# Blocks of tokens backwards in the second half of each layer, and the weights' lower halves on VectorE

## The chip, the cores and the metric

The kernel runs on one core of a Trainium2 chip. The metric is device time in microseconds (us), the median of three runs. A profile is taken of one further execution; its views count from the first instruction (the span).

## The reference

Linear attention, then two gated feed-forward layers one after the other, all in float32:

```python
def phi(x):                                  # per head, 128 features
    proj = x @ w_phi
    proj = proj - max(abs(proj), over features)
    return concatenate([exp(proj), exp(-proj)])
q_p, k_p = phi(q), phi(k)                    # 4 batches, 8 heads, 576 tokens, 64 wide
x = (q_p @ (k_p^T v)) / (q_p @ sum(k_p) + 1e-6)      # 2304 tokens x 512
x = (silu(x @ w_gate)     * (x @ w_val))  @ w_out    # layer 1, 512 -> 1536 -> 512
x = (sigmoid(x @ w_gate2) * (x @ w_val2)) @ w_out2   # layer 2
```

## The kernel before

**Arithmetic.** A float32 matmul is made of three matmuls of a shorter float type: each operand is cut into an upper half (a cast) and a lower half (the source minus the upper half), and upper x upper, upper x lower and lower x upper are summed in PSUM. Cutting one operand is therefore a cast on ScalarE and a subtraction on another engine; `halves` (line 196) does both. The gate and value products go by Strassen's scheme with 7 block products instead of 8, so that weights and tokens first go through sums of quarters (`sums`, on VectorE), and the results are put together by ScalarE copies (`keep`) and VectorE additions (`add`).

**Staging.** Each layer is run in two halves of 768 hidden columns, so there are four of them, `hh` = 0 to 3, and three turns between them: 0 to 1 and 2 to 3 inside a layer, 1 to 2 from layer to layer. In each half the loop runs over five blocks of tokens (`BLOCKS`: four of 512 and, in third place, one of 256) and inside a block over three pairs of weight columns (`p` = 0, 1, 2). One (hh, block, p) is a unit. Within a unit of a full block the order of the products is `ORDER[1]` = 1, 5, a, b, 6, 3, c, 7, 2, d, 4. The digits are Strassen products (each 2 x 6 matmuls of 256 columns); the letters are the output matmuls (`accumulate`) of the unit before, in four groups of six matmuls of 512 columns, `a` and `b` for its first hidden part (f = 0), `c` and `d` for its second (f = 1).

**PSUM hand-overs.** Products 1, 6, 7 and 4 add up in one bank (tag `a`). ScalarE must have copied it after 1 and after 6 (`keep`) before the next of them may write, and VectorE must have added it after 7 (`add`, line 634, `c<-a,c`) before 4 may write. The output sums of a block stay in the four banks of tags `c` and `d` until `out_sum` empties them.

**What a turn brings.** The halves of three weight pairs are kept on the chip in two tiles per pair (`w0h`, `w0l` and so on, with `o0h`, `o0l` for the output weights). When a unit is the last reader of its pair, `plan_slot` loads the pair of the next half (`a<-wf`, `o0l<-wfo`), sums and cuts it. In turn 0 to 1, 1 to 2 and 2 to 3 the subtraction of the 1024-wide weight piece is on VectorE, and those of the 768-wide one (the Strassen sums, source `s`) and of the output weights are on GpSimd (`SE`, line 814). Tokens have two buffers (`x0`, `x1`); before each block `plan_x_block` loads it (`b<-xo`), sums (lines 568 to 571) and cuts it (`xl`). In the first half of a layer each block's output sums are copied out and stored (`part<-o`); in the second they are loaded back (`o<-part`) and added.

**Order.** Every step has a planned time (`at(t, ...)`), steps are written in the order of these times, and a scheduling layer then sets the order on each engine. On the chip an engine runs its instructions strictly in that order. DMAs are all issued from SyncE's one queue, in order too. Loads and stores share four staging buffers (`piece`, tag `raw`).

Of the kernel before, what the change touches and what calls it, by code (L numbers as in the profile page):

```python
# [58 lines left out]
BLOCKS = [(0, 512), (512, 512), (2048, 256), (1024, 512), (1536, 512)]  # L59
NPAIR = 3  # L60


# [44 lines left out]
def body(ctx: ExitStack, tc: tile.TileContext, qT, kT, v, w_phi2, wpk, out):  # L107
# [87 lines left out]

    def halves(eng, hi, lo, src, act):
        act = act or anchor["early"]
        with tc.issue_after(anchor["act" if act else "dve"].ins):
            (nc.scalar.copy if act else nc.vector.tensor_copy)(hi, src)  # L199
        eng.tensor_tensor(out=lo, in0=src, in1=hi, op=ALU.subtract)  # L200

    def plan_slot(t, hh, p, eng, gap=3.0, out=14.0):
        l, q = hh // 2, (hh % 2) * NPAIR + p
# [18 lines left out]
        def split(w, m):  # L222
            if (hh, p) not in wts:
                wts[hh, p] = [pools[f"w{p}"].tile([P, 2, 2, 7, P], R32, tag=f"w{p}{x}",
                                                  name=f"w{p}{x}{hh}") for x in "hl"]
            d, src = ((slice(0, 4), a), (slice(4, 7), s))[m]
            halves(eng[m], *(x[:, w, :, d] for x in wts[hh, p]), src[w], WA)

# [7 lines left out]
        def split_out():  # L236
            hi, lo = wts[hh, p, "o"]
            halves(eng[2], hi, lo, lo.bitcast(F32), WA)

# [309 lines left out]

    def plan_x_block(t, hh, j, eng, gap):  # L550
        n = BLOCKS[j][1]
# [23 lines left out]
        def split(c, m):  # L575
            if (hh, j) not in xs:
                k = (hh * len(BLOCKS) + j) % 2
                xs[hh, j] = [pools[f"x{k}"].tile([P, 2, 7, NQ], R32, tag=x, name=x)
                             for x in ("xh", "xl")]
            d = ((slice(0, 4), slice(4, 7)) if full else (slice(0, 4, 2), slice(4, 5)))[m]  # L580
            src = b[c] if m == 0 else s[c][:, :3 if full else 1]
            halves(eng[m], *(x[:, c, d] for x in xs[hh, j]), src, XA)

# [6 lines left out]
    def product(r, hh, j, p, w, k):  # L590
# [12 lines left out]
        a, b = (PROD if full else PROD_HALF)[k]  # L603
        wh, wl = (x[:, w, :, a] for x in wts[hh, p])
        xh, xl = (x[:, :, b] for x in xs[hh, j])
        for c in range(2):
# [58 lines left out]
    def accumulate(r, hh, j, p, f, h):  # L665
        n = BLOCKS[j][1]
        wh, wl = (x[:, f] for x in wts[hh, p, "o"])
        uh, ul = r["u", f]
        m = (KC if hh < 2 else n // P) // 2
        for i in range(h * m, h * m + m):  # L670
            if p == 0 and f == 0:
                acc[hh, j, i] = bank(tags[i])
            ps = acc[hh, j, i]
            for m, (a, x) in enumerate(((wh, uh), (wh, ul), (wl, uh))):
                st, sp = p == 0 and f == 0 and m == 0, p == NPAIR - 1 and f == 1 and m == 2
                k = slice(i * P, (i + 1) * P)
                if hh < 2:
                    nc.tensor.matmul(ps[:, :n], a[:, k], x, start=st, stop=sp)  # L678
                else:
                    nc.tensor.matmul(ps, x[:, k], a, start=st, stop=sp)  # L680

    def out_banks(hh, j, k):
# [18 lines left out]
    def out_sum(hh, j, k):  # L701
        o, _ = out_tile(hh, j, k)
        banks, w = out_banks(hh, j, k)
        for m, i in enumerate(banks):
            ps = acc[hh, j, i][:, :w]
            if hh % 2 == 1:
                nc.vector.tensor_tensor(out=o[:, m], in0=ps, in1=o[:, m], op=ALU.add)
            elif m < OA:
                nc.scalar.copy(o[:, m], ps)
            else:  # L710
                nc.vector.tensor_copy(o[:, m], ps)
# [18 lines left out]
    def plan_out(t, r, hh, j, p, f, h):  # L730
# [3 lines left out]
        t += 6 * n / NQ * PT  # L734
        if p == NPAIR - 1 and f == 1:
            if hh < 2:
# [3 lines left out]
            for i, k in enumerate(tiles):  # L740
                if hh % 2 == 1:
                    at(t - 8.0, out_load, hh, j, k)
                at(t + 0.1 + 1.2 * i, out_sum, hh, j, k)
                at(t + OS + 1.5 * i, out_store, hh, j, k)
# [53 lines left out]
    for hh in range(4):  # L798
        begin.append(t)
        for j, (_, n) in enumerate(BLOCKS):  # L800
            if last:
                xprep.append((t, hh, j))
# [8 lines left out]

    S0 = X0 = (nc.vector,) * 3
    V, G = nc.vector, nc.gpsimd
    SE, XE = ((V, G, G), (V, G, G), (V, G, G)), (V, V)
    SG, XG = 2.72, 2.13
# [9 lines left out]
    for j, b in enumerate((0, 1, 3, 2, 3)):  # L825
        for c in range(2):
            plan_norm(ready[b] + NO[j] + 3.0 * c, j, c)
    plan_x_block(ready[0] + NO[0] + X00, 0, 0, X0, 3.0)
    plan_slot(T0 - WO, 0, 0, S0)
    plan_slot(ready["e"] + W1, 0, 1, S0, 1.5)  # L830
    plan_slot(ready["nd"] + W2, 0, 2, (G, G, G))
    for t, hh, j in xprep:
        plan_x_block(t - XL, hh, j, XE, XG)
    for hh in range(1, 4):
        plan_rounds(hh, begin[hh - 1] + RA, begin[hh] - RZ)
        for p in range(NPAIR):
            plan_slot(free[hh - 1, p] + SO, hh, p, SE[p], SG)
    plan.issue()
# [42 lines left out]
```

## Time and profile before

| | |
|---|---|
| median of three runs | 1072.55 us (1068.43 to 1075.91) |
| profiled execution, its own time | 1068.21 us |
| span of the profile | 1066.2 us |
| mean granted TensorE clock over the span | 0.992 |
| TensorE matmul busy | 1023.8 us, 96% |
| VectorE busy | 747.3 us, 70% |
| ScalarE busy | 556.9 us, 52% |
| GpSimd busy | 128.9 us, 12% |

Attention takes about the first 190 us of the span, the two layers the rest. In the views, PE is TensorE, PEld its weight loads, DVE VectorE, ACT ScalarE, POOL GpSimd, SP SyncE; L200 is line 200. A share of busy time is a mean over stages: for the layers read it turn by turn. The granted clock 1.00 is 2.4 GHz and 0.50 is 1.2 GHz.

### The profile page before, as it was taken

The numbers are of one execution on the slowest core, as the hardware profiler recorded it, in microseconds if no ns is written. First come the engines' busy times: TensorE is split into PE (matmuls) and PEld (weight loads), VectorE is DVE, ScalarE is ACT, GpSimd is POOL, SyncE is SP. The second block draws the span as 40 slices with busy tenths as digits, with TensorE's granted clock in tenths as the row PEclk, the third lists the DMA queues.
The fourth block names the chain that finished last, engine by engine and source line by source line (L and its number), as shares of the span: only waits on it lengthen the run. The fifth ranks groups of instructions, "written<-read, shape, count | busy, mean of one in ns | idle before, by whom it ended". The sixth has DMA issues, their size and how long they took to land.

```text
span 1066.2 us, 20722 instructions
## 1 busy us (share of the span) xinstructions
PE 1023.8 (96%) x8344; PEld 918.8 (86%) x8344; DVE 747.3 (70%) x1274; ACT 556.9 (52%) x1006; POOL 128.9 (12%) x109
## 2 busy tenths in 40 slices
PE   7999999997999998999999999999999899999998
PEld 6777776786999888999998888999989799999997
DVE  6988888875766788667757887567577974563433
ACT  5887877633555555534444455465455453332322
POOL 3322330210000014200000133000001230000000
PEclk9999999998999999999999999999999999999999
DMA  7777867648756251436634534154434340340111
GB/s 226 218 242 209 240 191 212 207 137 240 241 169 178 89 190 44 154 110 207 218 130 141 174 111 158 52 188 161 138 116 159 99 144 15 104 134 34 47 40 40
DMA packets 88575, 157.41 MB, mean 148 GB/s; under 512 B 28896, under 2 KB 50592, under 8 KB 88480
## 3 DMA queue, kind: packets, MB, share of 16 engines
q1 hardware_dynamic: 88480, 156.10, 46.9%
q8 instruction: 65, 1.06, 0.4%
q14 instruction: 30, 0.25, 0.1%
HBM read 108.73 MB, written 47.33 MB: 146 GB/s over the span
## 4 chain that ended last, share of the span: by engine, by line
PE 70%; DVE 13%; DMA 10%; ACT 3%; issue 2%; SPq 1%; POOL 0%; DVEq 0%; ACTq 0%
PE a L608 21%; PE b L608 15%; PE c L680 7%; PE d L680 5%; PE d L678 5%; PE c L678 5%; PE d L412 4%; PE a L317 4%; DMA rb<-rden 3%; DMA raw<-wpk 3%; PE c L363 3%; DVE xl L200 2%; DMA b<-xo 1%; DVE c L634 1%; PE b L385 1%
## 5 line engine op out<-in xcount | busy, mean ns | idle before, releaser
L646 ACT ACTIVATE c<-c 128x256 f32<-128x256 f32 x96 | 50.2, 524 | 166.6 <-DVE c L634 166.5
L659 DVE TENSOR_TENSOR ul<-c,uh 128x512 fp32r<-128x512 f32 (+1 forms) x120 | 75.1, 636 | 49.7 <-ACT uh L658 49.0
L628 ACT COPY c<-a 128x512 f32<-128x512 f32 x96 | 56.1, 584 | 86.8 <-PE a L608 77.4
L658 ACT CAST uh<-c 128x512 fp32r<-128x512 f32 (+1 forms) x120 | 68.5, 576 | 61.5 <-DVE c L651 53.6
L634 DVE TENSOR_TENSOR c<-b,c 128x512 f32<-128x512 f32 x96 | 65.6, 684 | 48.9 <-PE b L608 48.9
L608 PE MATMUL a<-xh,w2h 128*128 128x256 f32 x288 | 82.0, 285 | 8.3 <-DVE c L634 8.3
L608 PE MATMUL a<-xh,w1h 128*128 128x256 f32 x288 | 81.5, 283 | 7.2 <-DVE c L634 7.2
L608 PE MATMUL a<-xh,w0h 128*128 128x256 f32 x288 | 81.0, 281 | 1.4 <-ACT c L628 1.4
L608 PE MATMUL a<-xh,w2l 128*128 128x256 f32 x288 | 81.5, 283 | 0.0
L608 PE MATMUL a<-xl,w2h 128*128 128x256 f32 x288 | 81.5, 283 | 0.0
L608 PE MATMUL a<-xh,w1l 128*128 128x256 f32 x288 | 81.0, 281 | 0.0
L608 PE MATMUL a<-xl,w1h 128*128 128x256 f32 x288 | 80.9, 281 | 0.0
L608 PE MATMUL a<-xh,w0l 128*128 128x256 f32 x288 | 80.5, 279 | 0.0
L608 PE MATMUL a<-xl,w0h 128*128 128x256 f32 x288 | 80.4, 279 | 0.0
L163 ACT ACTIVATE raw<-raw 128x512 int32<-128x512 uint32 x72 | 48.7, 678 | 60.1 <-DMA raw<-wpk 54.6
L651 DVE TENSOR_TENSOR c<-c 128x256 f32<-128x256 f32 x96 | 56.3, 586 | 28.4 <-ACT c L646 27.7
L200 POOL TENSOR_TENSOR w0l<-s,w0h 128x768 fp32r<-128x768 f32 x6 | 12.4, 2059 | 501.0 <-PE b L608 333.3
L167 DVE TENSOR_SCALAR wcv<-wcv 128x512 f32<-128x512 f32 x72 | 32.3, 449 | 54.7 <-ACT wcv L160 54.6
L608 PEld LDWEIGHTS a<-xh,w2h 128*128 128x128 f32 x288 | 55.6, 193 | 11.8 <-DVE c L634 9.6
L200 DVE TENSOR_TENSOR xl<-b,xh 128x1024 fp32r<-128x1024 f32 (+1 forms) x40 | 50.7, 1267 | 20.1 <-ACT xh L199 19.9
L608 PEld LDWEIGHTS a<-xh,w1h 128*128 128x128 f32 x288 | 54.8, 190 | 11.5 <-DVE c L634 9.3
L608 PE MATMUL b<-xh,w1h 128*128 128x256 f32 x224 | 62.3, 278 | 0.0
(181 smaller groups left out, 3500.5 us busy)
## 6 DMA issues: line engine op xcount, KB each, us to landing
raw<-wpk SPq DMA_DIRECT2D x72, 512.0 KB
b<-xo SPq DMA_DIRECT2D x32, 512.0 KB
wf<-wcv SPq DMA_DIRECT2D x48, 256.0 KB
a<-wf SPq DMA_DIRECT2D x24, 512.0 KB
part<-o SPq DMA_DIRECT2D x17, 512.0 KB
o<-part SPq DMA_DIRECT2D x17, 512.0 KB
wfo<-wcv SPq DMA_DIRECT2D x24, 256.0 KB
x<-kT SPq DMA_DIRECT2D x18, 256.0 KB
```

The lines of the kernel that those rows point to most:

```text
L163: nc.scalar.activation(r["lo"].bitcast(I32), r["lo"], AF.Copy, scale=2.0 ** -29)
L200: eng.tensor_tensor(out=lo, in0=src, in1=hi, op=ALU.subtract)
L317: nc.tensor.matmul(ps[:, i * 256:(i + 1) * 256], x[:, i, o:o + P], w, start=(m == 0 and i == 0), stop=(m == 2 and i == 1), skip_group_chec ...
L608: nc.tensor.matmul(o, f[:, c], x[:, c], start=k == first and w == 0 and c == 0 and m == 0, stop=c == 1 and m == 2, skip_group_check=True)
L628: anchor["act"] = nc.scalar.copy(part_of(r, d), parts(r, src))
L634: anchor["dve"] = nc.vector.tensor_tensor(out=c, in0=parts(r, "zy x"[d]), in1=c, op=ALU.add)
L646: nc.scalar.activation(o, g, AF.Silu if hh < 2 else AF.Sigmoid)
L651: nc.vector.tensor_tensor(out=o, in0=v, in1=places(r, j, 0, d)[1], op=ALU.mult)
L658: nc.scalar.copy(hi, v)
L659: nc.vector.tensor_tensor(out=lo, in0=v, in1=hi, op=ALU.subtract)
L678: nc.tensor.matmul(ps[:, :n], a[:, k], x, start=st, stop=sp)
L680: nc.tensor.matmul(ps, x[:, k], a, start=st, stop=sp)
```

## The change

`ROUTE` orders the blocks 0, 1, 2, 3, 4 in halves 0 and 3 and 4, 3, 2, 1, 0 in halves 1 and 2. So the last two blocks of half 0 (3 and 4) are the first two of half 1, in reverse, and so for halves 2 and 3; their cut tokens are still in the two buffers and are used again (`xs[hh, j] = None`). The block at the turn also keeps its output sums in PSUM (`goes_on`): no copy, no store and no load of `part` for it. The turn from layer 1 to layer 2 (1 to 2) prepares its blocks as before. `halves` loses its engine argument: every lower half of tokens and weights is now subtracted on VectorE.

```diff
+ROUTE = ((0, 1, 2, 3, 4), (4, 3, 2, 1, 0), (4, 3, 2, 1, 0), (0, 1, 2, 3, 4))
...
-    def halves(eng, hi, lo, src, act):
+    def halves(hi, lo, src, act):
...
-        eng.tensor_tensor(out=lo, in0=src, in1=hi, op=ALU.subtract)
+        nc.vector.tensor_tensor(out=lo, in0=src, in1=hi, op=ALU.subtract)
...
-                k = (hh * len(BLOCKS) + j) % 2
+                k = (hh // 2 + ROUTE[hh].index(j)) % 2
...
+        if xs[hh, j] is None:
+            xs[hh, j] = xs[hh - 1, j]
...
+            begins, ends = not goes_on(hh, j), not goes_on(hh + 1, j)
             if p == 0 and f == 0:
-                acc[hh, j, i] = bank(tags[i])
+                acc[hh, j, i] = bank(tags[i]) if begins else acc[hh - 1, j, i]
...
+    def goes_on(hh, j):
+
+        return hh % 2 == 1 and ROUTE[hh][0] == j == ROUTE[hh - 1][-1]
...
-            if hh % 2 == 1:
+            if hh % 2 == 1 and not goes_on(hh, j):
                 nc.vector.tensor_tensor(out=o[:, m], in0=ps, in1=o[:, m], op=ALU.add)
...
-        if p == NPAIR - 1 and f == 1:
+        if p == NPAIR - 1 and f == 1 and not goes_on(hh + 1, j):
...
-                if hh % 2 == 1:
+                if hh % 2 == 1 and not goes_on(hh, j):
                     at(t - 8.0, out_load, hh, j, k)
...
-        for j, (_, n) in enumerate(BLOCKS):
-            if last:
+        for i, j in enumerate(ROUTE[hh]):
+            if hh % 2 == 1 and i < 2:
+                xs[hh, j] = None
+            elif last:
                 xprep.append((t, hh, j))
...
-    S0 = X0 = (nc.vector,) * 3
-    V, G = nc.vector, nc.gpsimd
-    SE, XE = ((V, G, G), (V, G, G), (V, G, G)), (V, V)
...
-    plan_slot(ready["nd"] + W2, 0, 2, (G, G, G))
+    plan_slot(ready["nd"] + W2, 0, 2)
```

The order of the matmuls on TensorE stays the same but for two places where three or four of them change places with their neighbours. Three places on VectorE and ScalarE follow. Line numbers in the rows of the changed kernel are its own: L203 there is L200 here, L220 to L223 are L217 to L220, L639 is L634, L656 is L651, L664 is L659, L543 is L540, L202 is L199, L651 on ScalarE is L646, L633 is L628, L663 is L658. In all names `w0` is the weight pair, `x` and `b` tokens, `s` and `t` Strassen sums, `c` a result in the making.

First place: VectorE at the turn 0 to 1, in the unit in which pair 0 of the next half is cut. Before:

```order
L569 TENSOR_TENSOR b<-b 128x256
L570 TENSOR_TENSOR t<-b 128x256
L571 TENSOR_TENSOR t<-b,t 128x256
L634 TENSOR_TENSOR c_5123<-b,c_5123 128x2x256
L568 TENSOR_TENSOR t<-b 128x256
L200 TENSOR_TENSOR w0l_5170<-a,w0h_5169 128x2x512
L200 TENSOR_TENSOR xl<-b,xh 128x1024
L634 TENSOR_TENSOR c_5139<-a,c_5139 128x2x256
```

In this order a token cut (`xl`) stands right ahead of the addition `c_5139<-a` that product 4 waits for. The same place after the change:

```order
L222 TENSOR_TENSOR s<-s,a 128x2x128
L223 TENSOR_TENSOR s<-a,s 128x2x128
L203 TENSOR_TENSOR w0l_5170<-s,w0h_5169 128x2x384
L639 TENSOR_TENSOR c_5123<-b,c_5123 128x2x256
L203 TENSOR_TENSOR w0l_5170<-a,w0h_5169 128x2x512
L203 TENSOR_TENSOR w0l_5170<-s,w0h_5169 128x2x384
L639 TENSOR_TENSOR c_5139<-a,c_5139 128x2x256
```

The tokens' four sums and cut are gone; sums of the next pair and two 768-wide weight subtractions stand in their place.

Second place: VectorE at the turn 1 to 2, one unit later, where pair 1 is cut. Before:

```order
L200 TENSOR_TENSOR xl<-b,xh 128x1024
L200 TENSOR_TENSOR xl<-t,xh 128x768
L200 TENSOR_TENSOR w1l_7666<-a,w1h_7665 128x2x512
L634 TENSOR_TENSOR c_7613<-b,c_7613 128x2x256
L217 TENSOR_TENSOR s<-a 128x2x128
L200 TENSOR_TENSOR w1l_7666<-a,w1h_7665 128x2x512
L218 TENSOR_TENSOR a<-a 128x2x128
L219 TENSOR_TENSOR s<-s,a 128x2x128
L634 TENSOR_TENSOR c_7632<-a,c_7632 128x2x256
```

Here the cuts of tokens and weights share the unit, and the output weights' subtraction is not on this engine. After the change:

```order
L203 TENSOR_TENSOR o0l_7507<-o0l_7507,o0h_7506 128x1024
L203 TENSOR_TENSOR xl<-b,xh 128x1024
L223 TENSOR_TENSOR s<-a,s 128x2x128
L203 TENSOR_TENSOR xl<-t,xh 128x768
L203 TENSOR_TENSOR w1l_7604<-a,w1h_7603 128x2x512
L639 TENSOR_TENSOR c_7551<-b,c_7551 128x2x256
L203 TENSOR_TENSOR w1l_7604<-s,w1h_7603 128x2x384
L221 TENSOR_TENSOR a<-a 128x2x128
L222 TENSOR_TENSOR s<-s,a 128x2x128
L639 TENSOR_TENSOR c_7570<-a,c_7570 128x2x256
```

The subtraction of `o0l`, which waits for a load and a cast, now stands at the head of this row, and one 1024-wide weight subtraction has moved behind the addition `c_7570<-a`.

Third place: VectorE near the start of the layers, where the last token block is normalised (`xraw`, which waits for the load of `rb`) beside the fifth or so unit. Before:

```order
L651 TENSOR_TENSOR c_3619<-c_3619 128x512
L540 TENSOR_TENSOR xraw<-xraw,rb 128x1024
L659 TENSOR_TENSOR ul_3749<-c_3619,uh_3748 128x512
L651 TENSOR_TENSOR c_3634<-a,c_3634 128x256
L659 TENSOR_TENSOR ul_3785<-c_3634,uh_3784 128x512
```

Both lower halves that the output matmuls read (`ul`) stand behind `xraw`. After the change:

```order
L656 TENSOR_TENSOR c_3619<-c_3619 128x512
L179 ISA wcv<-raw,wcv 128x1024
L656 TENSOR_TENSOR c_3634<-a,c_3634 128x256
L664 TENSOR_TENSOR ul_3749<-c_3619,uh_3748 128x512
L543 TENSOR_TENSOR xraw<-xraw,rb 128x1024
L664 TENSOR_TENSOR ul_3785<-c_3634,uh_3784 128x512
```

The first `ul` has moved ahead of `xraw`, the second still stands behind it.

## Rows read from the trace of the kernel before

**Rows 1.** The page, busy time, share of the span, instructions of each engine.
```profile
PE 1023.8 (96%) x8344; PEld 918.8 (86%) x8344; DVE 747.3 (70%) x1274; ACT 556.9 (52%) x1006; POOL 128.9 (12%) x109
```

**Rows 2.** Windows at the turns: length, busy us by engine (instructions), clock, DMA share, GB/s.
```profile
380.00:420.00 40.00, 34.99 (x234) 31.82 (x234) 35.11 (x55) 20.83 (x32) 12.78 (x5) 0.96 0.37 119
600.00:640.00 40.00, 35.61 (x242) 32.62 (x241) 33.54 (x49) 21.61 (x32) 13.10 (x6) 0.96 0.40 131
820.00:860.00 40.00, 34.75 (x235) 31.85 (x235) 34.71 (x51) 22.70 (x33) 14.04 (x7) 0.96 0.26 81
```

**Rows 3.** Waits of TensorE from 240 us: us in total, times, longest.
```profile
PE a L608 <- DVE c L634: 14.2, 6, 3.1
```

**Rows 4.** Timeline, VectorE at turn 0 to 1: start, us, instruction, [idle before <- releaser].
```profile
386.40 0.42 DVE L569 TENSOR_TENSOR b<-b 128x256 f32<-128x256 f32 x1
...
389.49 0.42 DVE L568 TENSOR_TENSOR t<-b 128x256 f32<-128x256 f32 x1 [1.15 <-POOL w0l L200]
...
390.97 2.87 DVE L200 TENSOR_TENSOR xl<-b,xh 128x1024 fp32r<-128x1024 f32 x1
393.77 0.68 DVE L634 TENSOR_TENSOR c<-a,c 128x512 f32<-128x512 f32 x1
...
406.34 2.87 DVE L200 TENSOR_TENSOR w1l<-a,w1h 128x1024 fp32r<-128x1024 f32 x1
...
409.73 1.46 DVE L217 TENSOR_TENSOR s<-a 128x256 f32<-128x256 f32 x1
...
412.92 0.68 DVE L634 TENSOR_TENSOR c<-a,c 128x512 f32<-128x512 f32 x1
```

**Rows 5.** Timeline, GpSimd at turn 0 to 1.
```profile
390.03 2.73 POOL L200 TENSOR_TENSOR w0l<-s,w0h 128x768 fp32r<-128x768 f32 x1 [0.57 <-ACT w0h L199]
...
405.61 5.30 POOL L200 TENSOR_TENSOR w1l<-s,w1h 128x768 fp32r<-128x768 f32 x2 [1.15 <-ACT w1h L199]
```

**Rows 6.** Timeline, TensorE at turn 0 to 1, the two product 4 that waited.
```profile
394.50 0.39 PE L608 MATMUL a<-xh,w1h 128*128 128x256 f32 x1 [1.51 <-DVE c L634]
...
413.65 0.38 PE L608 MATMUL a<-xh,w2h 128*128 128x256 f32 x1 [3.07 <-DVE c L634]
```

**Rows 7.** Line 200 on VectorE: ns minimum, median, maximum of each subtraction.
```profile
L200 DVE TENSOR_TENSOR xl<-b,xh x40: 682/1216/2879, 177.7 to 1000.8; 128x1024 fp32r<-128x1024 f32 x32, 128x512 fp32r<-128x512 f32 x8
...
L200 DVE TENSOR_TENSOR w0l<-s,w0h x2: 944/946/948, 158.2 to 170.5; 128x768 fp32r<-128x768 f32 x2
```

**Rows 8.** Chain of waits, turn 0 to 1: one product, one output group.
```profile
370.49 1.41 PE b L608 x12
371.90 1.39 PE c L678 x6
```

**Rows 9.** Chain of waits, turn 2 to 3: loads and the cast behind one.
```profile
813.31 5.04 DMA a<-wf
...
829.12 7.37 DMA o0l<-wfo
...
836.51 1.05 ACT o0h L199
837.56 0.95 ACT xh L199
```

**Rows 10.** Chain of waits, turn 1 to 2: the tokens' way through memory.
```profile
594.16 5.69 DMA xo<-o
599.87 4.94 DMA b<-xo
```

**Rows 11.** Timeline near the start of the layers, all engines.
```profile
260.20 1.23 DVE L540 TENSOR_TENSOR xraw<-xraw,rb 128x1024 f32<-128x1024 f32 x1 [3.86 <-DMA rb<-rden]
...
261.34 0.68 DVE L659 TENSOR_TENSOR ul<-c,uh 128x512 fp32r<-128x512 f32 x1
...
262.08 0.79 PE L678 MATMUL c<-ul,o0h 128*128 128x512 f32 x1 [4.28 <-DVE ul L659]
```

**Rows 12.** Window near the start of the layers (columns of Rows 2).
```profile
254.00:274.00 20.00, 14.97 (x90) 13.43 (x89) 9.85 (x15) 8.40 (x16) 0.00 (x0) 0.83 0.86 258
```

More of the change, by code (lines that the diff above doesn't have):

```diff
@@ L199, in halves, with plan_slot @@
             (nc.scalar.copy if act else nc.vector.tensor_copy)(hi, src)
-        eng.tensor_tensor(out=lo, in0=src, in1=hi, op=ALU.subtract)
-    def plan_slot(t, hh, p, eng, gap=3.0, out=14.0):
+        nc.vector.tensor_tensor(out=lo, in0=src, in1=hi, op=ALU.subtract)
+    def plan_slot(t, hh, p, gap=3.0, out=14.0):
         l, q = hh // 2, (hh % 2) * NPAIR + p
@@ L226, in split @@
             d, src = ((slice(0, 4), a), (slice(4, 7), s))[m]
-            halves(eng[m], *(x[:, w, :, d] for x in wts[hh, p]), src[w], WA)
+            halves(*(x[:, w, :, d] for x in wts[hh, p]), src[w], WA)
         def load_out():
@@ L237, in split_out @@
             hi, lo = wts[hh, p, "o"]
-            halves(eng[2], hi, lo, lo.bitcast(F32), WA)
+            halves(hi, lo, lo.bitcast(F32), WA)
         for w in range(2):
@@ L548, in plan_norm, with plan_x_block @@
         at(t + 8.0, store)
-    def plan_x_block(t, hh, j, eng, gap):
+    def plan_x_block(t, hh, j, gap):
         n = BLOCKS[j][1]
@@ L581, in split @@
             src = b[c] if m == 0 else s[c][:, :3 if full else 1]
-            halves(eng[m], *(x[:, c, d] for x in xs[hh, j]), src, XA)
+            halves(*(x[:, c, d] for x in xs[hh, j]), src, XA)
         for c in range(2):
@@ L670, in accumulate @@
         for i in range(h * m, h * m + m):
+            begins, ends = not goes_on(hh, j), not goes_on(hh + 1, j)
             if p == 0 and f == 0:
-                acc[hh, j, i] = bank(tags[i])
+                acc[hh, j, i] = bank(tags[i]) if begins else acc[hh - 1, j, i]
             ps = acc[hh, j, i]
             for m, (a, x) in enumerate(((wh, uh), (wh, ul), (wl, uh))):
-                st, sp = p == 0 and f == 0 and m == 0, p == NPAIR - 1 and f == 1 and m == 2
+                st = begins and p == 0 and f == 0 and m == 0
+                sp = ends and p == NPAIR - 1 and f == 1 and m == 2
                 k = slice(i * P, (i + 1) * P)
@@ L827, in body @@
             plan_norm(ready[b] + NO[j] + 3.0 * c, j, c)
-    plan_x_block(ready[0] + NO[0] + X00, 0, 0, X0, 3.0)
-    plan_slot(T0 - WO, 0, 0, S0)
-    plan_slot(ready["e"] + W1, 0, 1, S0, 1.5)
-    plan_slot(ready["nd"] + W2, 0, 2, (G, G, G))
+    plan_x_block(ready[0] + NO[0] + X00, 0, 0, 3.0)
+    plan_slot(T0 - WO, 0, 0)
+    plan_slot(ready["e"] + W1, 0, 1, 1.5)
+    plan_slot(ready["nd"] + W2, 0, 2)
     for t, hh, j in xprep:
-        plan_x_block(t - XL, hh, j, XE, XG)
+        plan_x_block(t - XL, hh, j, XG)
     for hh in range(1, 4):
@@ L836, in body @@
         for p in range(NPAIR):
-            plan_slot(free[hh - 1, p] + SO, hh, p, SE[p], SG)
+            plan_slot(free[hh - 1, p] + SO, hh, p, SG)
     plan.issue()
```

## The prediction

> **What bounds the kernel now.** The busy times come first: TensorE works 96% of the span, VectorE 70%, GpSimd 12% [rows 1]. The matmuls are the same before and after, so the change can only win what TensorE loses by waiting or by a lower clock. Where that is, a table of windows tells: in the undisturbed stretches of the layers TensorE is busy all the time; at each turn, in 40 us, it is busy only 34.99, 35.61 and 34.75 us, and the granted clock is 0.96 instead of 1.00 [rows 2]. Idle time: 5.0 + 4.4 + 5.3 = 14.7 us. The clock: a mean of 0.96 is 0.04 x 40 = 1.6 us of full-speed work lost per turn, 4.8 us in all. Together 19.5 us is what the three turns cost. The list of waits names the releaser: of TensorE's waits from 240 us on, six, 14.2 us together, are for VectorE's addition at line 634, two per turn [rows 3]. They are all product 4 waiting for the addition after product 7 [rows 6].
>
> The timeline shows why the addition is late. VectorE's 1024-wide subtraction takes 1.22 us as a rule (the median is 1216 ns) but 2.87 us twice in this turn [rows 4, 7], and each time GpSimd is in its own subtraction [rows 5]; a quarter-wide sum goes from 0.42 to 1.46 us in the same way, and once VectorE waits 1.15 us for GpSimd outright [rows 4]. Three such stretches and the wait lie in the 24 us ahead of the two late additions: 2 x 1.65 + 1.04 + 1.15 = 5.5 us of VectorE time. So the turns are bound by VectorE, in part by its own work and in part by GpSimd standing in its way.
>
> A second place is the start of the layers: at 260 us VectorE sits 3.86 us before `xraw` until a load lands, the lower half `ul` stands behind it, and TensorE waits 4.28 us [rows 11]; the granted clock there is 0.83 over 20 us [rows 12].
>
> **The change, part by part.**
>
> *Tokens not prepared at turns 0 to 1 and 2 to 3.* Gone per turn, for two blocks of two pieces each: 16 sums of 0.42 us, 4 cuts of 1.22 and 4 of 0.95 us [rows 4, 7], which is 15.4 us of VectorE, 7.7 us of it (one block) in the two units that waited. The casts on ScalarE and four loads of 512 KB go too. In SyncE's queue the weights' loads move up into the places of the token loads. That shortens the wait; I cost it at nothing more.
>
> *PSUM kept over the turn.* Four copies, four additions, two stores and two loads fewer per layer. They lie beside TensorE's work a unit or more from any wait of rows 3: nothing gained, nothing lost.
>
> *Lower halves to VectorE.* Per turn six of 768 and three of 1024 come to VectorE: 6 x 0.95 + 3 x 1.22 = 9.4 us [rows 7], of which in the two units that waited 4 x 0.95 + 1.22 = 5.0 us. Against that stand the 5.5 us above, which end with GpSimd's work. So at turn 1 to 2, where the tokens are still prepared, VectorE's load stays about level; at the other two it falls by 7.7 + 5.5 - 5.0 = 8.2 us, from 35 of 40 us [rows 2] to about 27.
>
> *The two additions at turn 0 to 1, step by step.* First unit: before, `xl` started at 390.97 and the addition at 393.77 [rows 4]. In the new order the four sums that end near 386.40 + 3 x 0.42 = 387.7 are sums of weights, and then come 0.95, the addition after product 3 with 0.68, 1.22, 0.95 and the addition in question with 0.68: 392.2 [rows 4, 7]. Product 4 could have started at 394.50 - 1.51 = 393.0 [rows 6]. No wait is left. Turn 2 to 3 is alike.
>
> Second unit: now VectorE also takes `o0l`, which waits for its load and for a cast; ahead of it in time stands nothing that TensorE needs, behind it two weight subtractions and both additions. Let T be the start of the unit. Output weights can be loaded once their last reader, group d, is done, one product before T, so about T - 1.0. Product 7 starts at T + 4 x 1.41 + 3 x 1.39 = T + 9.8 (products 1, 5, 6, 3 and groups a, b, c), product 4 after products 7, 2 and group d at T + 14.0 [rows 8]. The load takes 5.04 us like its neighbour or 7.37 like the one at turn 2 to 3 [rows 9], which shared the queue with two others. With 7.37: cast done at T + 7.4, `w1h` cast T + 8.5, copy after product 6 done T + 9.1, ahead of product 7. VectorE: `o0l` T + 8.7, 1024 T + 9.9, 768 T + 10.9, addition T + 11.5, 1024 T + 12.7, 768 T + 13.6, the addition product 4 needs at T + 14.3: a wait of 0.3 us. With 5.04 none. I take 0.3 at each of these turns.
>
> *Turn 1 to 2.* The first unit: the tokens come by a store of 5.69 and a load of 4.94 us [rows 10], unchanged; without GpSimd's share the addition lies within a few tenths of product 4: no wait taken. The second unit: between the cast of `o0` and the copy after product 6 ScalarE still has two token casts of 0.95 us [rows 9], 1.9 us more. With 7.37 the copy ends at T + 11.0, 1.2 us after product 7 could start, and the addition for product 4 at T + 15.5. That is a wait of 1.5 us; with 4.94 none. I take 1.5, and keep 1.6 us of lower clock with it, since every turn with waits shows that loss [rows 2].
>
> By the Trainium skill (DMA: Bandwidth & Descriptors, section "Anatomy of one DMA — SWDGE (gpsimd) path") a transfer costs 2.0 us plus its bytes at 436 GB/s, an estimate of 3.2 us for 512 KB, stated for the other issuing path; by it no turn would keep a wait and the sum would be 1068.2 - 19.5 - 5 = 1043.7. The trace does not agree: its loads of that size take 4.94 to 7.37 us.
>
> *The start.* The first `ul` now stands ahead of `xraw`, the second behind. TensorE reads the second only after groups a, b and products 6, 3, that is 2 x 1.39 + 2 x 1.41 = 5.6 us [rows 8] after group a began, half a us ahead of its wait, at 257.3: at 262.9; `xraw` and `ul` end at 260.20 + 1.23 + 0.68 = 262.1. So the wait of 4.28 goes, and with it the clock's loss: 0.17 x 20 = 3.4 us, of which up to 4.28 / 2 = 2.1 fell on idle time, so 1.3, together 5.6. Bounds: 0, if the load of `rb` lands later or another instruction waits in its place, and 5.6. I take 5, near the upper end, since the order shows the step itself. Pair 2 of the first half (5.5 us of subtractions, now on VectorE) falls at 201 to 217 us, where GpSimd's hold was of the same size: nothing.
>
> **The sum.** Turns: 19.5 less 0.3 + 0.3 + 1.5 + 1.6 = 15.8 us won. Start: 5. 1068.2 - 20.8 = 1047.4 for an execution like the profiled one. That one lies 0.2 us under the lowest of the three runs and 4.3 under their median. Runs that lie higher probably lose it in the same waits, which are now fewer, so I add little of it: **1048 us**.
>
> **Rivals.**
> *The gain is given back at turn 1 to 2 and the start (partial).* VectorE there carries tokens and all weights in order; one cast that lands late delays everything behind. If turn 1 to 2 keeps its 6.5 us (a third of 19.5) and the start its 5: 1068.2 - 2 x 6.5 + 0.6 = 1055.8, with the runs' spread up to 1061. For it: VectorE is busy 33.5 of 40 us there already. Against it: GpSimd's hold is gone.
> *The turns are bound by loads, not by VectorE.* Chain pieces of loads end in the late stretches [rows 9, 10]. Then TensorE waits just as long for other instructions: 1064 to 1072. Against it: the loads' buffers come free earlier, and only one of the two waits per turn has a load in its chain.
> *VectorE and ScalarE stuck behind loads (slower).* GpSimd could wait for output weights at no cost; VectorE cannot. Nine such subtractions (o0, o1, o2 at three turns), and at turn 0 to 1 three raw weight pieces that ScalarE now handles ahead of gates, stand in order before TensorE's additions. Each us beyond T + 6.4 costs 1 us at each. To lose 1% beyond the 20.8 won, 31.5 us, the loads would have to take 7.4 + 31.5 / 9 = 10.9 us. The longest row is 7.37. Time then: 1079.
> *The change does less than it says,* since the scheduling layer sets the order: the order shows that GpSimd has no subtraction left in the layers, so this has no chance of its own.
>
> **How the numbers follow.** Within 1% is about what a measurement of this kernel can tell from no change: 1061.8 to 1083.3. Forecast 0.63 (1040 to 1052: all waits and the start gone, or the start's gain missing); partial 0.22 (1052 to 1061); bound by loads 0.11; stuck 0.04. So faster 0.85, same 0.11, slower 0.04. The range leaves out the last two cases: low 1039 (the sum less 3.7 us of waits kept, less the 0.6 between bound and value at the start, less the 4.3 us by which executions stood apart before), high 1061.
>
> **What would show it.** In the windows of the three turns TensorE should be busy over 39 of 40 us with a clock of 1.00 at the first and third. The list of waits should have no six waits for the addition. The 1024-wide subtraction should have a maximum near 1.23 us, GpSimd no subtraction after 175 us. The wait at 262 us should be gone. The prediction is wrong if TensorE waits for `c<-a` or for ScalarE's copy behind `o0h`, `o1h` at the turns, or if `xraw` holds another reader at the start.

## The result and the profile after

The changed kernel took 1046.72 us (median of 6 runs, 1041.87 to 1050.72), the kernel before 1070.93 us in the runs beside it (6 runs, 1068.43 to 1075.91). The ratio is 0.976 with a 95% interval of 0.9734 to 0.9786. The forecast was 1048 us and a range of 1039 to 1061.

The profiled execution of the changed kernel is the longest of its six, 1050.72 us with a span of 1048.9; that of before, with a span of 1066.2, was shorter than all of its timed runs. So the two profiles differ by 17.3 us where the medians differ by 24.2. The page's first part, after, answers to [rows 1]:

```profile
PE 1022.0 (97%) x8344; PEld 919.6 (88%) x8344; DVE 710.7 (68%) x1250; ACT 544.0 (52%) x990; POOL 52.8 (5%) x77
```

There are as many matmuls as before. GpSimd has lost 32 subtractions, but VectorE is busy for less: 710.7 instead of 747.3 us. It took over those 32 and has the tokens of two turns less; and in the layers nothing of GpSimd runs beside it any more.

The windows at the three turns come earlier now, since the gain adds up. Their columns are those of [rows 2], with which they are to be compared:

```profile
375.00:415.00 40.00, 40.00 (x277) 37.09 (x277) 31.16 (x56) 23.81 (x38) 0.00 (x0) 1.00 0.49 150
590.00:630.00 40.00, 40.00 (x279) 37.08 (x278) 37.49 (x67) 25.96 (x40) 0.00 (x0) 1.00 0.49 166
805.00:845.00 40.00, 38.94 (x275) 35.89 (x274) 31.39 (x54) 21.78 (x32) 0.00 (x0) 1.00 0.27 88
```

TensorE was idle for 14.7 us in the three windows of before; now it is for 1.06, and the clock is 1.00 where it was 0.96. These are 13.6 + 4.8 = 18.4 us won. The middle row is the one to look at: VectorE is busy 37.49 of 40 us there, more than in any window of before, and TensorE doesn't wait at all.

The list of TensorE's waits from 240 us on answers to [rows 3]:

```profile
PE a L613 <- DVE c L639: 2.4, 2, 1.4
PE b L613 <- ACT c L633: 2.1, 1, 2.1
PE c L685 <- ACT o L720: 1.7, 1, 1.7
PE c L687 <- ACT uh L663: 1.6, 1, 1.6
```

Six waits of 14.2 us for the addition after product 7 have become two, of which one (1.06 us at 817 us) is at a turn and the other at the start. The other rows are waits at the start, small ones at 349 us, and three of 2.8 us in all at 762 and 772 us, in the second block from the end of the third half. There ScalarE waits for raw weights (6.00 and 1.84 us), and its copy and cast come late. In the kernel before the waits at this place are 0.83 us, and the clock stays at 1.00. The windows, first before, then after, have the columns of [rows 2]:

```profile
770.00:810.00 40.00, 39.17 (x275) 35.88 (x274) 29.20 (x53) 18.50 (x33) 0.00 (x0) 1.00 0.34 107
```

```profile
755.00:795.00 40.00, 37.14 (x247) 33.23 (x246) 26.15 (x47) 17.09 (x30) 0.00 (x0) 0.96 0.32 99
```

The changed kernel loses 2.0 us of waits and 1.6 of clock more than before here. In its second execution (experiment 9) the waits here are 2.4 us and the clock stays at 1.00.

How the late addition came to be on time is in the timeline of VectorE at turn 0 to 1, which answers to [rows 4]. L639 is the addition, L203 the subtraction of a lower half:

```profile
387.60 0.95 DVE L203 TENSOR_TENSOR w0l<-s,w0h 128x768 fp32r<-128x768 f32 x1
388.46 0.68 DVE L639 TENSOR_TENSOR c<-b,c 128x512 f32<-128x512 f32 x1
389.06 1.21 DVE L203 TENSOR_TENSOR w0l<-a,w0h 128x1024 fp32r<-128x1024 f32 x1
390.20 0.95 DVE L203 TENSOR_TENSOR w0l<-s,w0h 128x768 fp32r<-128x768 f32 x1
391.07 0.68 DVE L639 TENSOR_TENSOR c<-a,c 128x512 f32<-128x512 f32 x1
...
403.75 1.22 DVE L203 TENSOR_TENSOR w1l<-a,w1h 128x1024 fp32r<-128x1024 f32 x1
404.88 0.95 DVE L203 TENSOR_TENSOR w1l<-s,w1h 128x768 fp32r<-128x768 f32 x1
405.75 0.68 DVE L639 TENSOR_TENSOR c<-a,c 128x512 f32<-128x512 f32 x1
```

The work stands back to back, as the prediction had put it together (0.95, 0.68, 1.22, 0.95, 0.68), and no operation is stretched. The additions end at 391.75 and 406.43; product 4 starts at 392.27 and 407.75, right behind the matmul before it. All of VectorE's 1024-wide subtractions show that, against [rows 7]:

```profile
L203 DVE TENSOR_TENSOR xl<-b,xh x32: 684/1218/1227, 179.4 to 983.6; 128x1024 fp32r<-128x1024 f32 x24, 128x512 fp32r<-128x512 f32 x8
...
L203 DVE TENSOR_TENSOR w1l<-a,w1h x8: 1215/1218/1224, 191.5 to 828.4; 128x1024 fp32r<-128x1024 f32 x8
```

The longest takes 1227 ns, where it was 2879.

At the start of the layers less was won. The timeline there, of VectorE, ScalarE and TensorE, answers to [rows 11]:

```profile
257.03 0.68 DVE L664 TENSOR_TENSOR ul<-c,uh 128x512 fp32r<-128x512 f32 x1
257.50 0.50 PE L685 MATMUL c<-uh,o0h 128*128 128x512 f32 x1 [1.71 <-ACT o L720]
260.21 1.23 DVE L543 TENSOR_TENSOR xraw<-xraw,rb 128x1024 f32<-128x1024 f32 x1 [2.51 <-DMA wf<-wcv]
261.14 0.67 ACT L163 ACTIVATE wcv<-raw 128x512 f32<-128x512 f32 x1 [2.20 <-DMA raw<-wpk]
262.77 0.39 PE L613 MATMUL b<-xh,w1h 128*128 128x256 f32 x1 [2.12 <-ACT c L633]
```

The first `ul` does go ahead of `xraw` now, and the wait of 4.28 us for it is gone. But ScalarE waits 2.20 us for raw weights, with copies behind it that TensorE needs, and TensorE stops twice, for 1.71 and 2.12 us.

### The profile page after: what moved, and what is told of

It reads as the page before. It is cut to its first block, busy times and chain, and to the rows that moved or that the text cites. A ratio compares the mean times of both kernels' runs of the same rounds, so it can differ in the third digit from the quotient of the medians.

```text
span 1048.9 us, 20556 instructions
## 1 busy us (share of the span) xinstructions
PE 1022.0 (97%) x8344; PEld 919.6 (88%) x8344; DVE 710.7 (68%) x1250; ACT 544.0 (52%) x990; POOL 52.8 (5%) x77
## 3 DMA queue, kind: packets, MB, share of 16 engines
q8 instruction: 65, 1.06, 0.4%
## 4 chain that ended last, share of the span: by engine, by line
PE 81%; DMA 9%; DVE 5%; ACT 2%; SPq 1%; issue 1%; DVEq 0%; ACTq 0%
PE a L613 25%; PE b L613 19%; PE c L687 7%; PE d L685 6%; PE c L685 6%; PE d L687 6%; PE a L320 4%; PE d L415 4%; PE c L366 3%; DMA rb<-rden 3%; DMA raw<-wpk 2%; DMA xo<-xraw 2%; PE b L388 1%; DMA a<-wf 1%; SPq L535 1%
## 5 line engine op out<-in xcount | busy, mean ns | idle before, releaser
L651 ACT ACTIVATE c<-c 128x256 f32<-128x256 f32 x96 | 50.3, 525 | 147.5 <-DVE c L639 147.5
L664 DVE TENSOR_TENSOR ul<-c,uh 128x512 fp32r<-128x512 f32 (+1 forms) x120 | 75.7, 636 | 51.5 <-ACT uh L663 50.7
L633 ACT COPY c<-a 128x512 f32<-128x512 f32 x96 | 56.1, 584 | 103.5 <-PE a L613 91.1
L639 DVE TENSOR_TENSOR c<-b,c 128x512 f32<-128x512 f32 x96 | 65.7, 684 | 48.9 <-PE b L613 45.5
L663 ACT CAST uh<-c 128x512 fp32r<-128x512 f32 (+1 forms) x120 | 68.7, 577 | 57.9 <-DVE c L656 53.2
L656 DVE TENSOR_TENSOR c<-c 128x256 f32<-128x256 f32 x96 | 53.1, 554 | 30.4 <-ACT c L651 30.2
L613 PE MATMUL b<-xh,w2l 128*128 128x256 f32 x224 | 62.2, 278 | 0.0
L613 PE MATMUL b<-xh,w1l 128*128 128x256 f32 x224 | 62.2, 278 | 0.0
L613 PE MATMUL b<-xh,w0l 128*128 128x256 f32 x224 | 62.2, 278 | 0.0
L613 PE MATMUL b<-xh,w2h 128*128 128x256 f32 x224 | 62.2, 278 | 0.0
```

The costliest lines, as they stand in the source:

```text
L613: nc.tensor.matmul(o, f[:, c], x[:, c], start=k == first and w == 0 and c == 0 and m == 0, stop=c == 1 and m == 2, skip_group_check=True)
L633: anchor["act"] = nc.scalar.copy(part_of(r, d), parts(r, src))
L639: anchor["dve"] = nc.vector.tensor_tensor(out=c, in0=parts(r, "zy x"[d]), in1=c, op=ALU.add)
L651: nc.scalar.activation(o, g, AF.Silu if hh < 2 else AF.Sigmoid)
L656: nc.vector.tensor_tensor(out=o, in0=v, in1=places(r, j, 0, d)[1], op=ALU.mult)
L663: nc.scalar.copy(hi, v)
```

## The experiments

Experiments 1 to 4, 5 to 8 and those of 9 were each run on one chip, beside the kernel before (medians there 1072.37, 1073.84 and 1072.81 us). Ratios are to those. Line numbers in rows are those of each kernel; names tell which line of the changed kernel it is.

**1. Only the move to VectorE.** One line of the kernel before is changed, and with it the subtractions of all lower halves; the order of blocks, the cutting of tokens at all turns and the way of the accumulators stay.

```diff
-    V, G = nc.vector, nc.gpsimd
+    V, G = nc.vector, nc.vector
```

> The lower halves on VectorE, with the block order of the kernel before: tokens are cut at all three turns and the accumulators go through memory. Theory of the prediction (GpSimd standing in VectorE's way is worth about as much as the subtractions it hands over): every turn is then like turn 1 to 2 of the changed kernel, which in the profile after has TensorE busy for 40.00 of 40 us, so no wait stays at any turn and the time is that of the changed kernel, 1045 to 1050 us. The prediction's own sum for that turn would keep 3.1 us at each, 3 x 3.1 = 9.3 instead of 3.7, so about 1052. Rival (at turns 0 to 1 and 2 to 3 the saved cutting of tokens is what wins): only turn 1 to 2 and the start gain, 7.5 + 3 us, so 1070.9 - 10.5 = 1060, with the waits for the addition still there at the other two turns.

Measured: 1046.89 us (5 runs), ratio 0.9741 (0.9715 to 0.9766). That is the whole gain, by one line. The windows at the turns:

```profile
375.00:415.00 40.00, 40.00 (x284) 37.35 (x283) 36.90 (x66) 25.40 (x40) 0.00 (x0) 1.00 0.40 139
590.00:630.00 40.00, 40.00 (x277) 36.98 (x276) 37.55 (x65) 26.17 (x37) 0.00 (x0) 1.00 0.47 157
805.00:845.00 40.00, 39.45 (x279) 36.10 (x278) 38.20 (x66) 26.58 (x41) 0.00 (x0) 1.00 0.33 105
```

VectorE is busy 36.90, 37.55 and 38.20 us of 40, more than in the kernel before (35.11, 33.54 and 34.71), and TensorE idles for 0.55 us in all. The rival, by which the saved tokens win at two of the turns, is out.

**2. Only the order of blocks.** The changed kernel, tokens saved and accumulators kept, with the lower halves on GpSimd where the kernel before had them.

```diff
+    def eng(hh, p, m):
+        return nc.gpsimd if (hh, p) == (0, 2) or hh and m else nc.vector
...
-        nc.vector.tensor_tensor(out=lo, in0=src, in1=hi, op=ALU.subtract)
+        eng.tensor_tensor(out=lo, in0=src, in1=hi, op=ALU.subtract)
```

> The new block order and the kept accumulators, with the lower halves on GpSimd as in the kernel before. Theory: at turn 1 to 2 nothing changes, so its two waits for the addition stay (7 us with the clock); at the other two turns VectorE has 15.4 us less to do and GpSimd still slows it, so waits there fall from 4.5 to 5.6 us to under 2 us each; the start keeps its loss of 3. Time 1070.9 - 2 x 5 = 1061, between 1057 and 1064. Rival (the hold by GpSimd is the whole matter): all turns keep their waits, 1068 to 1071. Rival (the saved cutting of tokens is the whole matter): 1070.9 - 2 x 7 = 1057 or less, and turn 1 to 2 the only one with waits.

Measured: 1071.12 us (12 runs), ratio 0.9973 (0.9951 to 0.9995). The theory's 1061 is out, the first rival holds: the reversed order by itself gives 0.3%. The windows, in the same stretches as [rows 2]:

```profile
380.00:420.00 40.00, 36.86 (x249) 34.05 (x249) 28.31 (x45) 19.80 (x33) 10.70 (x5) 0.96 0.40 136
600.00:640.00 40.00, 34.95 (x228) 31.50 (x227) 34.05 (x54) 21.16 (x32) 12.71 (x5) 0.96 0.42 137
820.00:860.00 40.00, 34.53 (x227) 31.49 (x226) 26.99 (x41) 17.60 (x27) 12.18 (x6) 0.96 0.24 80
```

VectorE's busy time falls from 35.11 to 28.31 us at the first turn and from 34.71 to 26.99 at the third, and TensorE still waits for it: six waits, 13.2 us, against 14.2 before. An engine with 12 of 40 us free and still late is not short of time there; it is waiting in a chain. The timeline of VectorE and GpSimd in the second unit of turn 0 to 1 shows the chain (L206 the lower halves, L223 to L226 the sums of weights, L642 the addition):

```profile
404.00 2.42 POOL L206 TENSOR_TENSOR o0l<-o0l,o0h 128x1024 fp32r<-128x1024 f32 x1 [11.02 <-ACT o0h L205]
404.90 2.59 DVE L206 TENSOR_TENSOR w1l<-a,w1h 128x1024 fp32r<-128x1024 f32 x1 [2.60 <-ACT w1h L205]
406.37 4.64 POOL L206 TENSOR_TENSOR w1l<-s,w1h 128x768 fp32r<-128x768 f32 x2
407.42 0.68 DVE L642 TENSOR_TENSOR c<-b,c 128x512 f32<-128x512 f32 x1
409.24 2.05 DVE L223 TENSOR_TENSOR s<-a 128x256 f32<-128x256 f32 x1 [1.15 <-POOL w1l L206]
411.21 1.21 DVE L206 TENSOR_TENSOR w1l<-a,w1h 128x1024 fp32r<-128x1024 f32 x1
...
413.02 0.68 DVE L642 TENSOR_TENSOR c<-a,c 128x512 f32<-128x512 f32 x1
```

`o0l` is in front on GpSimd, so `w1l` begins at 406.37. VectorE's 1024-wide operation beside `o0l` takes 2.59 us instead of 1.22. Then VectorE wants the scratch `s`, which GpSimd's first `w1l` still reads, and waits 1.15 us. Its next operation, a quarter-wide sum, takes 2.05 instead of 0.42 us beside the second `w1l`. The addition starts at 413.02. Fewer tokens on VectorE shorten none of this.

**3. Accumulators not kept.** The changed kernel with `goes_on` returning False, so that the block at turns 0 to 1 and 2 to 3 stores and reloads its sums.

```diff
-        return hh % 2 == 1 and ROUTE[hh][0] == j == ROUTE[hh - 1][-1]
+        return False
```

> The changed kernel, but the block at turns 0 to 1 and 2 to 3 gives its accumulators to memory and adds them again half a layer later, as the other blocks do; its split tokens are still used twice. Theory (these copies, additions, stores and loads lie beside TensorE's work): the time of the changed kernel, 1045 to 1050 us, no new wait over 0.5 us at the turns. Rival (two additions and two loads more fall into the units that waited): 1 to 2 us of wait at each of two turns with the clock's loss, 1050 to 1054 us.

Measured: 1043.09 us (4 runs, 1042.49 to 1044.91), ratio 0.9728 (0.9707 to 0.9749). The rival, by which storing them costs 3 us or more, is out. It even came out 3.6 us below the changed kernel; see 9 for whether that holds.

**4. The start's share.** The changed kernel with the lower halves of pair 2 of the first half on GpSimd (`eng` gives GpSimd for `(hh, p) == (0, 2)` alone).

> The changed kernel with the lower halves of pair 2 of the first half, the only ones that moved ahead of the first turn, back on GpSimd. Theory of the prediction (the start is worth 5 us, since the first lower half of the gated product goes ahead of the token scaling that waits for a load): 1046.7 + 5 = 1052, and a wait of some 4 us near 262 us again. By the profile after, in which the layers' first 100 us are only 3 us shorter than before, 1046.7 + 3 = 1050. Rival (the start's stops come and go by when loads land, whatever the order): within 1.5 us of the changed kernel, 1045 to 1048.5.

Measured: 1051.51 us (5 runs), ratio 0.9796 (0.9774 to 0.9817). That is 4.8 us above the changed kernel, near the prediction's 5; but the two were not run side by side, by their ratios it is 3.9 us, and the intervals touch. The wait is back, in TensorE's timeline:

```profile
264.66 0.80 PE L688 MATMUL c<-ul,o0h 128*128 128x512 f32 x1 [4.99 <-DVE ul L667]
```

**5. and 6. Which of GpSimd's subtractions hold.** The changed kernel with only the output weights' (`eng`: `hh and m == 2`), and with only the 768-wide ones (`hh and m == 1`) back on GpSimd.

> The changed kernel with only the output weights' lower halves of the second to fourth half-layer (o0l, o1l, o2l, three of 1024 per turn) back on GpSimd. Theory after the first four runs (the turns were held by GpSimd, in two ways: VectorE's operations with two inputs in SBUF take 1 to 1.7 us longer beside a GpSimd subtraction, and VectorE waits 1.15 us for GpSimd to give the scratch s back): the output weights need no scratch, so only the first way is there, once or twice per turn, 1.4 to 2.8 us, against 1.2 us that VectorE is spared in each unit; waits of at most 1 us per turn, time 1046 to 1050 us. Rival (any GpSimd subtraction in a unit makes the addition late): one wait of 1.5 to 2.5 us per turn, with 1.6 us of clock, 3 x 3.5 = 10, so 1055 to 1059 us.

> The changed kernel with only the 768-wide lower halves of the weights (six per turn) back on GpSimd; the output weights' stay on VectorE. Theory: these are the ones that read the scratch s, so both ways of the hold come back: two stretches of slowed VectorE operations and the 1.15 us wait in each of the two units, 2.2 to 3 us late per unit. Two waits per turn, 1062 to 1070 us. Rival (the output weights' subtraction, queued ahead of the second unit's on GpSimd, was what made that one late): waits only in the first unit of each turn, 3 x 2.5 us, 1053 to 1057 us.

Measured: 1046.78 us (6 runs, 0.9747, 0.9713 to 0.9782) with the output weights', 1057.56 us (4 runs, 0.9854, 0.9825 to 0.9882) with the 768-wide. TensorE's waits for the addition, first with the one, then with the other on GpSimd:

```profile
PE a L616 <- DVE c L642: 4.5, 3, 1.8
```

```profile
PE a L616 <- DVE c L642: 10.6, 8, 2.6
```

With the output weights' the theory's time holds; the waits are a little longer than it had them (1.78 us at turn 1 to 2 and 1.69 at 2 to 3; the third of the three is at the start). Only the first of them is new: at turn 2 to 3 the changed kernel itself waits 1.06 us, and 1.47 in its second execution. With the 768-wide the theory's waits hold, two at every turn, six of the eight, of 0.88 to 2.60 us, but not its time: they cost 11 us and not 15 to 23. The rival's time, 1053 to 1057 us, is nearer, but it had a wait in the first unit of each turn alone. Part of what is missing is the clock: with both back (experiment 2) it is 0.96 at every turn, with the 768-wide alone 1.00 at all three.

**7. A one-input operation on GpSimd.** The kernel before, with a copy in place of each of GpSimd's subtractions.

```diff
+        if eng is nc.gpsimd:
+            eng.tensor_copy(lo, src)
+        else:
+            eng.tensor_tensor(out=lo, in0=src, in1=hi, op=ALU.subtract)
```

> The kernel before, with each of GpSimd's subtractions of lower halves replaced by its plain copy of the same size from the full-precision piece to the lower half (one input; the subtraction is left out, the lower halves there are not what they should be). Block order, queues, scratch buffers and who waits for whom stay, except that the copy doesn't wait for the cast. Theory (it is the two-input operation on GpSimd that blocks VectorE's two-input operations): the 1024-wide subtraction on VectorE stays near 1.22 us beside it, and with a copy of well under 2.7 us the waits fall to under 1 us each: 1046 to 1055 us. Rival (what counts is that VectorE waits for scratch that GpSimd still reads, at whatever speed, or any GpSimd operation blocks VectorE): waits as before, 1065 to 1073 us.

Measured: 1053.38 us (5 runs), ratio 0.9804 (0.9776 to 0.9832). Its start is that of the kernel before (a wait of 3.9 us for `ul`), which experiment 4 puts at 5 us; so nearly all that the turns had to give is won. The one row of waits for the addition that is left:

```profile
PE a L611 <- DVE c L637: 0.3, 1, 0.3
```

The theory's time holds, its reason holds in part. GpSimd's line in the list of groups, first as this copy, then as the subtraction of experiment 6:

```profile
L201 POOL CAST w1l<-s 128x768 fp32r<-128x768 f32 x6 | 9.1, 1516 | 39.8 <-DVE s L223 39.8
```

```profile
L206 POOL TENSOR_TENSOR w1l<-s,w1h 128x768 fp32r<-128x768 f32 x6 | 12.6, 2128 | 39.3 <-ACT w1h L205 39.3
```

The copy is shorter and needs no cast first. But VectorE is still slowed beside it: a 1024-wide subtraction takes up to 2.02 us, a 768-wide up to 1.58 instead of 0.95. So it isn't the second input alone that stands in the way; the copy stands there for less long. The two (shorter hold, scratch back sooner) were not told apart.

**8. Stops put in by hand.** The changed kernel, with VectorE copying product 1's bank into product 5's ahead of it, at three units.

```diff
+            if k == 5 and p == 1 and (hh, ROUTE[hh].index(j)) in ((1, 1), (1, 3), (2, 1)):
+                nc.vector.tensor_copy(r[at_k], r["x"])
```

> The changed kernel with three stops of TensorE put in by hand, in the second and fourth block of the second half and the second block of the third half: there VectorE copies the bank of product 1 into the bank of product 5 ahead of it, so that product 5 waits for it (the copied numbers are overwritten). In the profiles so far TensorE's 256-wide products follow each other at 113.4 or at 117.8 ns, for 50 to 280 us at a stretch, and the spacing changes mostly at stops. Theory (a restart sets the spacing): within a unit of each of the three stops the spacing changes in at least one case, in stretches where the profile after has one spacing from 353 to 626 us; each stop costs 1 to 1.5 us, so 3 to 4.5 us less up to 6 us of spacing: 1043 to 1052 us. Rival (the spacing belongs to the place in the program): 117.8 ns from 353 to 626 us again, whatever the stops, and 1050 to 1052 us.

Measured: 1043.27 us (4 runs), ratio 0.9715 (0.9689 to 0.9741). The stops didn't come about: an output group went ahead of product 5 and covered the copy, so the longest was 0.3 us. The spacing was 113.4 ns in most of the stretch where the profile after has 117.8, which the rival didn't expect, and the theory can't claim it either. Inconclusive; the last section has what it adds.

**9. The raw weights of the second half later, and the changed kernel again.** The steps that prepare them begin 70 instead of 44.6 us after the layers' start, in the version of experiment 3 and in the changed kernel.

```diff
-        plan_rounds(hh, begin[hh - 1] + RA, begin[hh] - RZ)
+        plan_rounds(hh, begin[hh - 1] + (70.0 if hh == 1 else RA), begin[hh] - RZ)
```

> The version without kept accumulators, with the preparation of the second half's raw weights begun 70 instead of 44.6 us after the layers' start (its 18 steps pressed into 105 instead of 131 us). In that version TensorE still loses 5.9 us between 245 and 280 us, where ScalarE and VectorE wait for raw weights that share the queue with the tokens' loads (idle 5.34, 3.07 and 2.52 us for them). Theory (these steps are what is late there): most of the 5.9 us go, 1 us comes back where the steps are denser: 1043.1 - 4 = 1039 us, between 1036 and 1041. Rival (the token loads are late by themselves): 1042 to 1046 us.

> The changed kernel, with its kept accumulators, and with the same later start of the second half's raw weights as in the kernel beside it. Theory: it gains the same 3 to 5 us at the start, 1046.7 - 4 = 1042.5 us; whether accumulators are kept makes no difference beyond what the spacing does, so it lies within 4 us of the kernel beside it. Rival (keeping them costs something): 3 to 4 us above the kernel beside it in every round, as in the first runs (1046.7 against 1043.1).

> The changed kernel once more, unchanged. In every profile so far the layers take 817.8 us (one 818.5) plus three sums: TensorE's longer spacing of products (7.4 to 14.1 us), its stops (11.8 to 35.6) and the stretches of half clock (1.5 to 7.8); the changed kernel had 10.5, 19.1 and 2.9. Theory (the spacing is left to chance at each stop, so it differs between executions of one program): the share of 117.8 ns products in this profile differs from 0.43 by more than 0.05, in other stretches, and the times spread over 1041 to 1051 us again; median 1046.7 within 3. Rival (the program fixes it): 0.43 in the same stretches, 353 to 626 us at 117.8 ns.

Measured, on one chip: 1043.57 us (6 runs, 1041.39 to 1049.56, ratio 0.9735) without kept accumulators, 1044.63 (6 runs, 1038.87 to 1047.99, 0.9726) with them, 1046.17 (6 runs, 1041.97 to 1048.03, 0.9741, 0.9706 to 0.9777) for the changed kernel itself. The first is no better than without the later start (1043.09). TensorE's waits of that version from 240 to 400 us:

```profile
PE c L685 <- ACT uh L663: 2.6, 2, 2.1
PE a L613 <- DVE c L639: 1.1, 1, 1.1
PE c L685 <- DVE ul L664: 0.9, 4, 0.2
```

In the version of experiment 3 the same list adds up to 4.7 us; here it is 4.6. The wait for ScalarE's copy `o` (2.7 us) is gone, a wait of 2.1 us for the cast `uh` has come in its place, and stops of 1.1 and 0.5 us at 340 and 361 us, probably from the denser steps. So the expected 4 us went into new waits.

By the times, what keeping the accumulators costs is not settled: 3.6 us in the first runs, 1.1 in these, with ranges that overlap. The profiles show one cost, at turn 2 to 3. In both pairs that differ in nothing else, TensorE waits there for the addition in the kept version (1.06 us in the changed kernel, 1.47 when run again, 1.65 with the later raw weights) and not at all in the other. What VectorE waits for ahead of it is a load of weights, first in the changed kernel, then in experiment 3:

```profile
808.90 0.43 DVE L220 TENSOR_TENSOR s<-a 128x256 f32<-128x256 f32 x1 [2.91 <-DMA a<-wf]
```

```profile
801.91 0.43 DVE L220 TENSOR_TENSOR s<-a 128x256 f32<-128x256 f32 x1 [0.42 <-DMA a<-wf]
```

In both the load is issued right behind the same store, at 802.24 and at 797.75 us, but it is waited for until 6.7 us later in the first and 4.2 in the second. In all six profiles of the changed kernel and its variants that keep the accumulators (experiments 4, 5 and 8 too) the load takes 6.3 to 7.3 us to land and TensorE waits 0.70 to 1.69 us; in the two that don't keep them (experiment 3, and 9 without) it takes 4.1 and 5.2 us and there is no wait. Why the load takes longer stays open. No version beats the changed kernel by more than such differences; the simplest that reaches it is experiment 1.

## Why the prediction was right, and where it was not

*The time* (1048 against 1046.7) and the range hold, and so do most of the signs that were named: no six waits, a longest subtraction of 1227 ns, GpSimd's last at 174.5 us, the wait of 4.28 us at 262 us gone. Two do not at turn 2 to 3: TensorE is busy for 38.94 and not over 39 of 40 us there, and it waits once for `c<-a`, which was named as a sign of being wrong.

That the sum came out near is in part luck. For the profiled execution it had 20.8 us; the two profiled executions differ by 17.5 (1068.21 and 1050.72). The turns gave 18.4 (forecast 15.8). The start gave 2.8 (forecast 5): TensorE is idle for 1.1 us less from 186 to 300 us, and the stretch of half clock there is 3.4 instead of 6.8 us long, which is 1.7 us of work. The third half took back 3.6 at 762 to 776 us, where nothing was forecast. What is left about cancels, and the other executions of the changed kernel were shorter than the profiled one.

*The turns.* The sum had 15.8 of 19.5 us won there; the windows show 18.4. The 3.1 us kept at turn 1 to 2 (1.5 for a late cast, 1.6 of clock) were not there: the second unit begins at 605.15 us, the cast of `o0` is done at 610.49, 5.3 us into it and not 7.4, which rested on the longest load among the rows. At turn 2 to 3 it was 1.06 us instead of 0.3, and in the first unit, for which the prediction had none: VectorE waits there for a load of weights until 808.90 us (2.91 us), and the addition that follows ends at 817.00, when product 4 could have started 1 us before. The profiles of experiment 9 lay that on the kept accumulators, which the prediction had at nothing. VectorE's load at turns 0 to 1 and 2 to 3 fell to 31 of 40 us and not to 27. Nor does every turn with waits lose clock, as the prediction had it: experiment 6 waits 2.2 to 3.8 us per turn at a clock of 1.00.

*Who held the turns* is the step that failed, though the time came out. The prediction said that the turns are bound by VectorE, in part by its own work, and it credited 7.7 us per turn to tokens that need not be cut. Experiment 1 cuts them all and has the same time; experiment 2 cuts none at two turns and has 0.3%. Saved tokens were worth nothing measurable, and kept accumulators cost a wait. GpSimd was the whole matter, by a chain that the prediction had in its rows (2.87, 1.46, the wait of 1.15) but set beside VectorE's own work as one of two terms of like size. At the turn where it left VectorE's load level it had to forecast what was left over, and was wrong by 3.1 us; at the others two terms stood for one, which the limit (a wait can't shrink below nothing) hid. With the order alone as the change, the same working would have been wrong by 10 us (1061 in the expectation of experiment 2, measured 1071).

By the Trainium skill (SBUF — State Buffer, section "SBUF: two separate sides") GpSimd and VectorE share one pair of ports, which one operation has for its whole length while the other is blocked, and a VectorE operation with two inputs in SBUF is among those that need it beside a GpSimd operation that reads SBUF. The traces agree as far as they go: 2.87, 2.59 and 2.05 us beside a GpSimd subtraction, never above 1.23 without one, and VectorE's additions with an operand in PSUM stayed at 0.68. The `xl` of 2.87 us [rows 4, 5] and the `w1l` of 2.59 us (experiment 2) end 1.08 and 1.07 us after the GpSimd subtraction beside them, little less than the 1.22 us that they take alone, as if they had begun when it ended.

*The start.* 5 us was near in size (3.9 to 4.8 by experiment 4, 2.8 between the two profiles), but not as worked out. The wait of 4.28 us went, and 1.71 + 2.12 us of waits for ScalarE came in its place, as the lower bound had it ("another instruction waits in its place"). Part of the rest came from where the prediction had put nothing: pair 2, on GpSimd from 203 to 219 us in experiment 4. There TensorE waits 0.69, 1.18 and 1.26 us between 207 and 221 us, in the changed kernel once, for 0.47.

*The rivals.* None of the three gave the time, but each has its place in the profile after: the start gave part of its gain back to ScalarE's waits, the 1.06 us at turn 2 to 3 go back to a load, and VectorE does wait 1.32 us for the cast behind `o0l` at 399.03 and at 824.28 us, without making TensorE late.

## What to carry to other kernels

A busy share tells whether an engine has time left, not whether it is on time: here the helper that took 12% of the load made its neighbour late, and VectorE at 38 of 40 us without GpSimd was on time where at 27 of 40 with it it was not. When an operation's longest duration is twice its median, look for what ran beside it, and price the whole chain (stretched operation, buffer given back late, next stretched operation) before the work that is saved. Of a change with two parts, run each alone: one line gave all of it.

## What the runs showed of the hardware that was not expected

TensorE's matmuls of 256 columns follow each other at one of two spacings, 113.4 or 117.8 ns, at the full clock and with no wait in between. It shows in the chain of waits, where a product of 12 matmuls takes 1.36 or 1.41 us. First the kernel before, then the changed one, in the same stretch and both fully busy:

```profile
433.40 1.36 PE b L608 x12
434.76 1.39 PE c L678 x6
```

```profile
431.83 1.41 PE b L613 x12
433.24 1.39 PE c L685 x6
```

Later it is the other way round (at 665 us the kernel before has 1.41). Up to some 650 us one spacing lasts for up to 346 us (299 to 646 us in experiment 4) and changes mostly at a stop, but not always. Taken from the starts of neighbouring matmuls behind the layers' first gate, 0.25 to 0.58 of some 4,700 had the longer one: 0.31 in the kernel before, 0.42 in the changed one, 0.58 in experiment 1, 0.25 in experiment 8. At 4.4 ns each the last two differ by 0.33 x 4,700 x 4.4 ns = 6.8 us, and their profiled spans by 6.2 (1045.8 and 1039.6) with TensorE's stops alike (13.0 and 13.5 us by the same starts); experiment 8 had 6.8 us of half clock at the start where experiment 1 had 3.4. So a gain of that size came and went between versions that differ little, and part of the changed kernel's spread, 1041.9 to 1050.7 us, is probably of this kind.

The place in the program doesn't fix these stretches: the same kernel had 117.8 ns from 353 to 626 us in one execution and 113.4 from 563 us on in the other. Behind 660 us the place does fix it in these two: the longer spacing stands behind 373 of 382 and 371 of 377 matmuls that are among the first five after an output group, and behind none of the 1,626 others. The expectation had the share differ by over 0.05; it was 0.42 and 0.46. What sets the long stretches stays open: nothing here tells a stop that changes the spacing from one that doesn't.
